# Splitting the second expert's first matrix during the routing, with its lower halves on GpSimd, and putting the last two attention outputs ahead of the transposes

## The chip, the core and the metric

The kernel runs on one core of a Trainium2 chip. Its engines work side by side: TensorE (PE, with its weight loads as PEld), VectorE (DVE), ScalarE (ACT), GpSimd (POOL) and SyncE (SP, which only issues transfers here). The metric is device time in microseconds (us), the median of several runs. Lower is better.

## The reference

```python
# attention: B, H, S, D = 4, 8, 768, 48
cur = einsum('bhd,bhe->bhde', u * kt, vt)
y[:, :, t] = einsum('bhd,bhde->bhe', rt, state + cur)
state = w * state + einsum('bhd,bhe->bhde', kt, vt)
# mixture of experts: 3072 tokens of 384 values, 8 experts, 384 tokens each
logits = x @ w_gate
...   # greedy: largest logit first, each token once, each expert at most 384 tokens
out[mask] = relu(x[mask] @ w1[e]) @ w2[e]
# dense part, on every token
h = maximum(maximum(x @ v1, x @ v2), x @ v3)
out = h @ w_out
```

The outputs of the attention are the rows x. Which expert gets a row depends on the logits of all 3072 rows, so no expert can start before the attention and the routing are over.

## The kernel before, in words

**Attention (`Attention.run`).** 24 steps, one for each block of 128 positions of one batch. A step `i` works on several blocks at once: it loads block i+4 (SP), lets GpSimd scale three operands of the blocks ahead (`decayed` L129, `natural` L184, `bonus` L192 and L193), transposes keys (`turn`, L213), makes the score matrix of block i+1 (`scores`: PE writes pA at L227, DVE masks it into am at L230), takes block i-1 through PE transposes into xt (`cross`: PE L302, ACT L304 and L305), issues four matmuls on ones that nobody reads (`keep`, L237), makes the output of block i (`rows`: PE writes pY at L248, DVE adds two halves into x at L263), adds the logits of block i-2 (`gate`, L313) and updates the state (`state`, L281 and L285, not in the last four steps). pA and pY have two buffers each per pair of tiles, pX has one. After the loop come `cross(23)`, `gate(22)`, `gate(23)` and the copy of all logits into raw (ACT, L359).

**Side work (`Feed`).** The weights are split into an upper and a lower f16 half. The work for this is a list of small pieces with a cost each, and four slots of every step take pieces as fast as the list is due (`due` spreads the summed cost over the steps). One matrix of an expert (`weight`) gives four pieces that sum squares (`look`, ACT L623), three that turn the maximum into a scale, and seven (first matrix) that split: piece n lets ACT write the upper half of part n (`upper`, L690) and DVE the lower half of part n-1 (`lower`, L694, one scalar_tensor_tensor: raw * s - upper, on 128x512). The list of the attention ends with the first matrix of expert 1, `X.weight(1, 0)`, so its six lower halves come last. The raw weights lie in four staging buffers; a load into one waits until its last reader is done.

**Routing (`Routing`).** Three rounds and `settle`, one chain of small DVE, PE and ACT instructions on a table of 128x192 logits, at whose end stand the ids (L1347), by which POOL gathers the rows (L876). At the end of a round `aside` takes pieces from the second list (`Experts.plan`): two, two and none, all `look` pieces of the second matrix of expert 1. In `settle` POOL multiplies into col (L1328) and makes five of the 24 row matrices (L1339).

**Experts (`Experts.run`).** For each expert four products on PE (L919, L1014), with the remaining side work in slots `side`. Each takes from a budget `feed.spare`, from which every piece that runs takes its cost (`Feed.run`); `flush` runs everything that must be done by then. Before the third product of expert 0 the last dense matrix, V[2] (`double(2)`), must be split: ACT L788, DVE L791.

Of the kernel before, what the change touches and what calls it, by code (L numbers as in the profile page):

```python
# [12 lines left out]
OP = mybir.AluOpType  # L13
# [7 lines left out]
NT = B * NC  # L21
# [16 lines left out]
KEEP = 4  # L38
# [6 lines left out]
class Attention:  # L45
# [270 lines left out]
    def run(self, feed):  # L316
        nc = self.nc
        self.load(3)
        feed.ahead(2)
        for i in range(2):  # L320
            self.turn(i)
        self.scores(0)
        self.extra(0)
        for i in range(NT):
            if i == 2:
                self.routing.prepare()

            def side(j):
                if i:
                    feed.spare = 0.0  # L330
                    feed.take(9, min(0.9, feed.due((4 * (i - 1) + j) / (4 * (NT - 4)))), j)

            self.load(i + 4)
            self.across(i + 3)
            self.store(i - 1)
            self.decayed(i + 2)
            self.natural(i + 3)
            self.bonus(i + 2)
            side(1)
            self.turn(i + 2)  # L340
            self.fade(i - 1)
            side(2)
            self.scores(i + 1)
            self.extra(i + 1)
            side(3)
            self.cross(i - 1)
            self.keep(KEEP)
            self.rows(i)
            self.gate(i - 2)
            side(4)  # L350
            self.state(i)
        while feed.left(9):
            feed.run()
        self.store(NT - 1)
        self.cross(NT - 1)
        self.gate(NT - 2)
        self.gate(NT - 1)
        K = self.K
        nc.scalar.activation(K.raw, self.lg, AF.Copy, scale=-1.0)  # L359
# [232 lines left out]
class Experts:  # L592
# [53 lines left out]
    def mark(self, st):  # L646
        st["sent"] = self.feed.now

    def weight(self, e, which, routed=False):

        nc = self.nc
        st = {"sent": 0.0}
        if which == 0:
            src, kb, n, store = self.w1d, self.KD, F, self.W1
            blocks = [self.block(src, e * DM * F + j * 512, [[F, 128], [128 * F, kb], [1, 512]], False)
                      for j in range(2)]
        else:
            src, kb, n, store = self.w2d, self.KF, DM, self.W2
            blocks = [self.block(src, e * DM * F + j * 4 * 128 * DM, [[DM, 128], [128 * DM, 4], [1, DM]], False)
                      for j in range(2)]  # L660

        def look(j):
            def go():
                if j == 0:
                    st["peaks"] = self.wp.tile([128, 4], F32, name=f"wpeak{which}")
                self.square(blocks[j // 2].get()[:, j % 2 * 768:j % 2 * 768 + 768], st["peaks"][:, j:j + 1])
                if j == 3 and not (self.early or routed):
                    self.mark(st)
            return go

        def column(out):
            nc.vector.tensor_reduce(out, st["peaks"], AX.X, OP.max)

        def powers(top):
            yield from self.sc.powering(top, 3, True, st)
            st["w"] = self.wpool[e % 2].tile([128, 2, kb, n], F16, name=f"w{which}", bufs=1)
            store[e] = (st["w"], st["f"])

        def part(j, q):
            if which == 0:  # L680
                return blocks[j].get()[:, q * 512:q * 512 + 512], [st["w"][:, t, q, j * 512:j * 512 + 512] for t in range(2)]
            k = 4 * j + 2 * q
            return blocks[j].get()[:, q * 768:q * 768 + 768], [
                st["w"][:, t, k:k + 2].rearrange("p k n -> p (k n)") for t in range(2)]

        parts = [(j, q) for j in range(2) for q in range(3 - which)]

        def upper(n):
            raw, (hi, _) = part(*parts[n])
            nc.scalar.activation(hi, raw, AF.Copy, scale=st["s"])  # L690

        def lower(n):
            raw, (hi, lo) = part(*parts[n])
            nc.vector.scalar_tensor_tensor(lo, raw, st["s"], hi, op0=OP.mult, op1=OP.subtract)  # L694

        def split(n):
            def go():
                if n < len(parts):
                    upper(n)
                if n:  # L700
                    lower(n - 1)
            return go

        def uses(n):
            return [blocks[parts[i][0]] for i in (n - 1, n) if 0 <= i < len(parts)]

        looks = [(look(j), False, [blocks[j // 2]], 0.9) for j in range(4)]
        if routed:
            self.later = lambda: self.across(column, powers)
        return (looks + ([] if routed else self.scaled(st, column, powers, blocks))  # L710
                + [(split(n), st if n == 0 and not self.early else False, uses(n), 0.6 + 0.3 * which)
                   for n in range(len(parts) + 1)])

    def double(self, i):

# [129 lines left out]
    def plan(self, late):  # L845

        feed = self.feed = Feed(12)
        self.early = False
        parts = [(0.2, self.weight(1, 1, True), None)] + [(1, self.double(i), 0) for i in late]
        parts[-1] = (1, parts[-1][1] + [(self.common, False, [], 1.5)], None)  # L850
        parts.append((1.5, self.double(3), 0))
        for e in range(2, E):
            parts += [(e, self.weight(e, 0), 7), (e + 0.3, self.weight(e, 1), 6)]
        feed.chain(parts)
        feed.close()
        feed.fill()

    def open(self, ctx):
# [259 lines left out]
class Routing:  # L1118
# [88 lines left out]
    def round(self, src, T, n=0):  # L1207

        nc, psum, RW, J, nl = self.nc, self.psum, self.RW, self.J, self.nl
# [38 lines left out]
        for n0, n1, a, c in ((0, V, -1.0, float(N - CAP)), (V, 2 * T, -2.0, float(2 * (N - CAP) - (J * W - 1)))):  # L1248
            nc.vector.tensor_scalar(goal[:RW, n0:n1], po[:RW, 32:33].to_broadcast([RW, n1 - n0]), a, c, op0=OP.mult,
                                    op1=OP.add)  # L1250
        junk = [self.small(f"junk{s}", [128, T + 2, J * W], BF16) for s in range(2)]
        rank = self.small("rank", [128, 2 * T])
        for a in range(2 * T):
            s, t = divmod(a, T)
# [3 lines left out]
            else:  # L1258
# [7 lines left out]
                                       op1=OP.is_equal, accum_out=pick[:RW, 1:2])  # L1266
# [7 lines left out]
                                       op1=OP.mult)  # L1274
        nc.tensor.matmul(pt[:, :E], pick[:RW, 0:1].to_broadcast([RW, 128]), self.same[:RW, :E], start=False, stop=True)
        self.idle(1 if src is self.K.raw else 3)
        self.aside((2, 2, 0)[n])
        pen = self.small("pen", [128, NT, E])
        nc.vector.tensor_tensor(pen, src, pt[:, None, :E].to_broadcast([128, NT, E]), OP.is_gt)
        nc.vector.scalar_tensor_tensor(nl, pen, BIG, src, op0=OP.mult, op1=OP.add)  # L1280
# [161 lines left out]
@with_exitstack  # L1442
def body(ctx, tc, r, rt, k, v, w, u, wg, w1, w2, v1, v2, v3, wo, out, dbg=None):
    nc = tc.nc
    ctx.enter_context(tc.manual_schedule())
    K = Consts(ctx, tc)
    dram = ctx.enter_context(tc.tile_pool(name="dram", bufs=1, space=DRAM))
    x_dram = dram.tile([N, DM], F32, name="x_rows")
    X = Experts(ctx, tc, K, w1, w2, (v1, v2, v3), wo, x_dram, out)
    routing = Routing(ctx, tc, K)  # L1450
    feed = Feed()
    for which in range(2):
        feed.add(0, X.weight(0, which))
    for i in EARLY:
        feed.add(0, X.double(i))
    feed.add(0, X.weight(1, 0))
    feed.close()
    with ExitStack() as actx:
        A = Attention(actx, tc, K, r, rt, k, v, w, u, wg, x_dram,
                      lambda: X.wp.tile([128, 1536], F32, name="stage", bufs=Feed.SLOTS), routing)  # L1460
        X.sc.psum = lambda: A.psum.tile([128, 3, C], F32, name="pX").rearrange("p j n -> p (j n)")
        A.run(feed)
    X.tokens(ctx)
    X.plan([i for i in range(3) if i not in EARLY])
    with ExitStack() as rctx:
        routing.run(rctx, X.inputs(), X.aside, X.sc, lambda: X.gather(0))
    X.open(ctx)
    X.run()
# [44 lines left out]
```

## Time and profile before

| | us |
|---|---|
| median of 3 runs | 688.36 |
| lowest, highest | 687.89, 694.27 |
| the profiled execution, its own time | 689.38 |
| its span, first to last instruction | 687.7 |
| PE busy | 646.8 (94%) |
| DVE busy | 398.8 (58%) |
| ACT busy | 352.2 (51%) |
| POOL busy | 243.6 (35%) |

The profiled execution takes 1.02 us more than the median; 1.68 us of its time lie outside the span. The attention reaches from 0 to about 161 us, the routing to 192 us (ids), the experts start their matmuls at about 197 us. Shares of busy time over the whole span mix these stages; the stages are to be read one by one.

### The profile page before, as it was taken

What the parts mean: (1) busy time and instruction counts of PE and PEld (TensorE: products, weight loads), DVE (VectorE), ACT (ScalarE), POOL (GpSimd) and SP (SyncE); (2) the same over time, 40 slices, a digit from 0 to 9 for tenths busy, and PEclk for the clock granted to TensorE, in tenths of its full rate; (3) what the DMA queues carried; (4) which work ended last, traced back from release to release, by engine and by line L of the source; (5) the groups of instructions that cost most, each with busy time, mean ns of one, the idle gap of its engine ahead of it and who ended that gap; (6) DMA issues with size and microseconds to landing.
All of it is one profiled execution on the core that took longest, in us unless ns stands there. A gap on an engine that the chain in (4) does not pass through costs nothing.

```text
span 687.7 us, 14407 instructions
## 1 busy us (share of the span) xinstructions
PE 646.8 (94%) x5670; PEld 430.1 (63%) x5670; DVE 398.8 (58%) x1048; ACT 352.2 (51%) x785; POOL 243.6 (35%) x270
## 2 busy tenths in 40 slices
PE   7899999997679998899999999999999999999996
PEld 5688787886466564456666656666665666666663
DVE  7787997785745757566366365544636544451321
ACT  3676566643444556466655655546454635442321
POOL 6899999970170003221022123102302111210222
PEclk9999999997569999999999999999999999999999
DMA  7986866615044309026237123412412210000100
GB/s 216 291 261 207 289 211 194 214 49 207 2 135 108 130 5 202 24 63 163 85 83 159 47 69 92 128 47 81 116 46 85 78 47 12 24 0 1 35 2 35
DMA packets 54764, 72.99 MB, mean 106 GB/s; under 512 B 21408, under 2 KB 42016, under 8 KB 54688
## 3 DMA queue, kind: packets, MB, share of 16 engines
q1 hardware_dynamic: 51616, 62.55, 30.6%
q0 software_dynamic: 3072, 9.44, 4.8%
q8 instruction: 46, 0.75, 0.5%
q14 instruction: 30, 0.25, 0.1%
HBM read 58.41 MB, written 9.44 MB: 99 GB/s over the span
## 4 chain that ended last, share of the span: by engine, by line
PE 54%; issue 8%; DVE 4%; ACT 3%; POOL 1%; POOLq 0%; DVEq 0%; ACTq 0%
PE pg L919 25%; PE ps L919 21%; PE px L1014 8%; ACT junk L623 1%; DVE top L996 1%; POOL gt L1001 1%; DVE x2s L977 1%; ACT w L690 1%; ACT gt L1000 0%; DVE ht L949 0%; DVE wo L791 0%; POOL out_dram L1019 0%; DVE gt L763 0%; DVE sc L430 0%; DVE da L747 0%
## 5 line engine op out<-in xcount | busy, mean ns | idle before, releaser
L919 PE MATMUL pg<-x2s,v 128*128 128x384 f16 x1296 | 217.5, 326 | 3.7 <-ACT top L994 3.1
L919 PEld LDWEIGHTS <-v 128*128 128x128 f16 x1296 | 126.8, 98 | 88.3 <-issue 4.8
L1001 POOL TENSOR_TENSOR gt<-top,gt 128x384 f16<-128x384 f32 x48 | 45.2, 941 | 343.5 <-ACT gt L1000 295.4
L919 PEld LDWEIGHTS <-w 128*128 128x128 f16 x1242 | 117.1, 99 | 72.2 <-issue 0.8
L694 DVE SCALAR_TENSOR_TENSOR w<-stage,sc,w 128x512 f16<-128x512 f32 (+1 forms) x80 | 72.7, 934 | 52.1 <-ACT w L690 52.1
L996 DVE SCALAR_TENSOR_TENSOR top<-pg,sc,top 128x384 f32<-128x384 f32 x96 | 59.0, 615 | 73.7 <-PE pg L919 63.6
L919 PE MATMUL ps<-ht,w 128*128 128x384 f16 x576 | 95.1, 326 | 0.1
L919 PE MATMUL ps<-xt,w 128*128 128x384 f16 (+1 forms) x540 | 88.6, 317 | 0.2 <-ACT xt L910 0.2
L1000 ACT ACTIVATE gt<-top 128x384 f16<-128x384 f32 x48 | 25.1, 522 | 111.5 <-DVE top L996 111.5
L1014 PE MATMUL px<-wo,gt 128*128 128x384 f16 x432 | 74.1, 331 | 4.5 <-ACT wo L788 1.6
L690 ACT ACTIVATE w<-stage,sc 128x512 f16<-128x512 f32 (+1 forms) x80 | 61.5, 798 | 6.1 <-DVE sc L468 6.1
L1014 PEld LDWEIGHTS <-gt 128*128 128x128 f16 x432 | 42.4, 99 | 35.1 <-issue 5.4
L623 ACT ACTIVATE junk<-stage 128x768 bf16<-128x768 f32 x64 | 53.6, 838 | 4.2 <-DMA stage<-in_moe_w_dram 3.3
L949 DVE SCALAR_TENSOR_TENSOR ht<-ps,ht 128x384 f16<-128x384 f32 x56 | 31.0, 555 | 32.3 <-ACT ht L948 32.3
L1019 POOL DMA_INDIRECT out_dram<-o,ids x24 | 23.9, 995 | 43.3 <-ACT o L1017 43.3
L994 ACT ACTIVATE top<-pg,sc 128x384 f32<-128x384 f32 x48 | 27.7, 577 | 19.0 <-PE pg L919 18.5
L960 ACT ACTIVATE x<-ps 128x384 f32<-128x384 f32 x24 | 11.8, 491 | 48.8 <-PE ps L919 48.8
L230 DVE TENSOR_TENSOR am<-pA,mask 128x512 f32<-128x512 f32 x48 | 30.7, 680 | 8.9 <-PE pA L227 8.9
L948 ACT ACTIVATE ht<-ps 128x384 f16<-128x384 f32 x56 | 26.8, 482 | 14.9 <-PE ps L919 14.4
L129 POOL TENSOR_TENSOR rt<-rt,tr 128x512 f32<-128x512 f32 x22 | 32.8, 1490 | 0.6 <-DMA rt<-in_rt_dram 0.6
L227 PE MATMUL pA<-rt,kt 64*128 64x128 f32 x384 | 31.9, 304 | 0.6 <-POOL rk L193 0.2
L1017 ACT ACTIVATE o<-px,sc 128x384 f32<-128x384 f32 x24 | 13.9, 580 | 36.1 <-PE px L1014 29.8
(235 smaller groups left out, 871.8 us busy)
## 6 DMA issues: line engine op xcount, KB each, us to landing
stage<-in_moe_w_dram SPq DMA_DIRECT2D x41, 768.0 KB, 5.2
kn<-in_k_dram SPq DMA_DIRECT2D x24, 192.0 KB, 5.2
rn<-in_r_dram SPq DMA_DIRECT2D x24, 192.0 KB, 5.4
v<-in_v_dram SPq DMA_DIRECT2D x24, 192.0 KB, 3.7
rt<-in_rt_dram SPq DMA_DIRECT2D x48, 96.0 KB, 3.6
x_rows<-x SPq DMA_DIRECT2D x24, 192.0 KB, 3.0
stage<-in_moe_w_out_dram SPq DMA_DIRECT2D x3, 768.0 KB, 6.0
xg<-x_rows,ids POOLq DMA_INDIRECT x24, 4.7
```

The source lines that it names most:

```text
L129: (engine or self.nc.gpsimd).tensor_mul(self.RT[i], self.RT[i], self.tr)
L227: nc.tensor.matmul(pa[s][:, j, :], kt[FULL[s], j * C:(j + 1) * C], rt[FULL[s], j * C:(j + 1) * C], start=True, stop=True, skip_group_check ...
L230: nc.vector.tensor_mul(am[:, s], pa[s], self.mask[:, None, :].to_broadcast([128, NP, C]))
L623: self.nc.scalar.activation(self.K.junk, x, AF.Square, accum_out=total)
L690: nc.scalar.activation(hi, raw, AF.Copy, scale=st["s"])
L694: nc.vector.scalar_tensor_tensor(lo, raw, st["s"], hi, op0=OP.mult, op1=OP.subtract)
L919: nc.tensor.matmul(p[:, rows], w[:, wi, k, cols], x[:, xi, k, rows], start=k == 0 and wi + xi == 0, stop=k == kb - 1 and xi == 1, skip_gro ...
L949: nc.vector.scalar_tensor_tensor(h[:, 1, f], p, 0.0, h[:, 0, f], op0=OP.max, op1=OP.subtract)
L994: nc.scalar.activation(t, p, AF.Copy, scale=self.ratio[i])
L996: nc.vector.scalar_tensor_tensor(t, p, self.ratio[i], top, op0=OP.mult, op1=OP.max)
L1001: nc.gpsimd.tensor_sub(gt[:, 1, g], top, gt[:, 0, g])
L1014: nc.tensor.matmul(p, gt[:, gi, g, a * 128:(a + 1) * 128], self.WO[:, wi, g, :], start=g == 0 and gi + wi == 0, stop=g == self.KG - 1 and ...
```

## The change

The pieces that split the first matrix of expert 1 leave the attention's list. `weight(1, 0, left=True)` keeps its looks and its scale there and puts the seven split pieces aside in `held`; `plan` inserts them into the second list behind its four looks, and gives the two staging buffers that hold this matrix to the second list. The rounds take 3, 4 and 4 pieces, so that the four looks and all seven split pieces run in the routing. The lower halves no longer are one DVE instruction each but two on GpSimd: a tensor_scalar that multiplies the raw weights in place, and a tensor_sub. In the attention's last two steps `rows(i)` stands before `cross(i-1)`, and `keep` is left out.

```diff
@@ Attention.run
-            self.cross(i - 1)
-            self.keep(KEEP)
-            self.rows(i)
+            if i < NT - 2:
+                self.cross(i - 1)
+                self.keep(KEEP)
+                self.rows(i)
+            else:
+                self.rows(i)
+                self.cross(i - 1)
             self.gate(i - 2)
@@ Experts.weight
-            nc.vector.scalar_tensor_tensor(lo, raw, st["s"], hi, op0=OP.mult, op1=OP.subtract)
+            if left:
+                nc.gpsimd.tensor_scalar(raw, raw, st["s"], None, op0=OP.mult)
+                nc.gpsimd.tensor_sub(lo, raw, hi)
+            else:
+                nc.vector.scalar_tensor_tensor(lo, raw, st["s"], hi, op0=OP.mult, op1=OP.subtract)
...
+        if left:
+            self.held, splits = (blocks, splits), []
+        return looks + ([] if routed else self.scaled(st, column, powers, blocks)) + splits
@@ Experts.plan
         feed.chain(parts)
+        blocks, splits = self.held
+        feed.plan[4:4] = [(0.1,) + x for x in splits]
+        for b in blocks:
+            b.first = None
         feed.close()
+        feed.blocks = blocks + [b for b in feed.blocks if b not in blocks]
+        feed.loaded = len(blocks)
         feed.fill()
@@ Routing.round
-        self.aside((2, 2, 0)[n])
+        self.aside((3, 4, 4)[n])
@@ body
-    feed.add(0, X.weight(1, 0))
+    feed.add(0, X.weight(1, 0, left=True))
```

DVE, the end of the attention, before (am: masked scores, bon: sums of the bonus, x: the output of a block, w: a half of the split matrix):

```order
L263 TENSOR_TENSOR x<-pY,bv 128x4x48 x2
L694 SCALAR_TENSOR_TENSOR w_2511<-stage,sc_2504,w_2511 128x512 x3
L230 TENSOR_TENSOR am<-pA,mask 128x512 x2
L201 TENSOR_REDUCE bon<-rk 128x8
L694 SCALAR_TENSOR_TENSOR w_2511<-stage,sc_2504,w_2511 128x512
L263 TENSOR_TENSOR x<-pY,bv 128x4x48 x2
L694 SCALAR_TENSOR_TENSOR w_2511<-stage,sc_2504,w_2511 128x512 x2
L230 TENSOR_TENSOR am<-pA,mask 128x512 x2
L201 TENSOR_REDUCE bon<-rk 128x8
L263 TENSOR_TENSOR x<-pY,bv 128x4x48 x4
```

and the same place of the change:

```order
L263 TENSOR_TENSOR x<-pY,bv 128x4x48 x2
L411 TENSOR_REDUCE sc_2566<-pX 1x1
L458 TENSOR_SCALAR sc_2581<-pX 128x1
L465 TENSOR_SCALAR sc_2585<-sc_2581 128x1
L467 TENSOR_SCALAR sc_2585<-sc_2585 128x1
L472 TENSOR_SCALAR sc_2583<-sc_2585 128x1
L472 TENSOR_SCALAR sc_2584<-sc_2585 128x1
L230 TENSOR_TENSOR am<-pA,mask 128x512 x2
L201 TENSOR_REDUCE bon<-rk 128x8
L263 TENSOR_TENSOR x<-pY,bv 128x4x48 x2
L230 TENSOR_TENSOR am<-pA,mask 128x512 x2
L201 TENSOR_REDUCE bon<-rk 128x8
```

The six lower halves between the last masks and outputs are gone; the seven small instructions that make the scale stand one step later than before.

PE, the last step of the attention and what follows it, before (pX<-identf,x: cross; lg<-onesf: keep, whose last pair is shown; pY: rows; lg<-wg: gate):

```order
L302 MATMUL pX<-identf,x 128x128 x3
...
L237 LDWEIGHTS onesf
L237 MATMUL lg<-onesf 128x256
L248 MATMUL pY<-S_119,rt_109 64x64 x16
L248 MATMUL pY<-v_123,am 64x64 x16
L313 MATMUL lg<-wg,xt 128x8 x3
L302 MATMUL pX<-identf,x 128x128 x3
L313 MATMUL lg<-wg,xt 128x8 x6
```

and of the change:

```order
L248 MATMUL pY<-S_119,rt_109 64x64 x16
L248 MATMUL pY<-v_123,am 64x64 x16
L302 MATMUL pX<-identf,x 128x128 x3
L313 MATMUL lg<-wg,xt 128x8 x3
L302 MATMUL pX<-identf,x 128x128 x3
L313 MATMUL lg<-wg,xt 128x8 x6
```

`rows(23)` now stands ahead of `cross(22)`, and the four keep matmuls are gone; step 22 changed in the same way.

POOL between the attention and `settle`, in the change (stage: the raw weights, w: the lower half; col: `settle`). Before, col followed bv directly:

```order
L203 TENSOR_TENSOR bv<-v_123,bon 128x384
L699 TENSOR_SCALAR stage<-stage,sc_2583 128x512
L700 TENSOR_TENSOR w_2590<-stage,w_2590 128x512
L699 TENSOR_SCALAR stage<-stage,sc_2583 128x512
L700 TENSOR_TENSOR w_2590<-stage,w_2590 128x512
...
L1344 TENSOR_TENSOR col<-col,tokf 128x6x24
L1355 TENSOR_SCALAR row<-i_150,bf,tokf 128x128 x5
```

Six such pairs stand there. On ACT the six upper halves (three at the end of the second round, three at the end of the third) and the looks, three and one instead of two and two, are all that the routing gains; on SP one load into a staging buffer fewer stands before the flag of the routing.

## Rows read from the trace of the kernel before

**Rows 1.** Windows by stage: bounds, length, engines' busy us (count), clock, DMA.

```profile
140.00:161.00 21.00, 19.94 (x377) 17.34 (x376) 14.49 (x29) 10.41 (x27) 11.78 (x11) 1.00 0.13 41
161.00:192.00 31.00, 19.85 (x107) 15.21 (x108) 21.81 (x120) 12.93 (x48) 4.57 (x6) 0.55 0.27 103
```

**Rows 2.** Timeline of PE, end of the attention: start, us, instruction, idle before.

```profile
145.07 1.16 PE L227 MATMUL pA<-rt,kt 64*128 64x128 f32 x16
...
148.78 0.84 PE L313 MATMUL lg<-wg,xt 128*128 128x8 f32 x6
149.84 1.55 PE L227 MATMUL pA<-rt,kt 64*128 64x128 f32 x16 [0.22 <-POOL rk L193]
151.97 0.52 PE L302 MATMUL pX<-identf,x 128*128 128x128 f32 x3 [0.59 <-DVE x L263]
152.33 0.60 PE L237 MATMUL lg<-onesf 128*128 128x256 bf16 x4
...
156.41 0.69 PE L248 MATMUL pY<-S,rt 64*64 64x64 f32 x32
...
159.05 0.52 PE L302 MATMUL pX<-identf,x 128*128 128x128 f32 x3
```

**Rows 3.** Timeline of DVE, same stretch.

```profile
144.52 4.46 DVE L694 SCALAR_TENSOR_TENSOR w<-stage,sc,w 128x512 f16<-128x512 f32 x3
148.90 1.27 DVE L230 TENSOR_TENSOR am<-pA,mask 128x512 f32<-128x512 f32 x2
...
151.22 0.61 DVE L263 TENSOR_TENSOR x<-pY,bv 128x192 f32<-128x192 f32 x2
151.75 1.44 DVE L694 SCALAR_TENSOR_TENSOR w<-stage,sc,w 128x512 f16<-128x512 f32 x2
```

**Rows 4.** Timeline of POOL, the same instruction without and beside L694 on DVE.

```profile
140.27 1.27 POOL L129 TENSOR_TENSOR rt<-rt,tr 128x512 f32<-128x512 f32 x1
...
145.29 1.72 POOL L129 TENSOR_TENSOR rt<-rt,tr 128x512 f32<-128x512 f32 x1
```

**Rows 5.** Timeline of DVE, early in the attention.

```profile
27.43 0.96 DVE L1190 TENSOR_SCALAR gone<-same 128x8 f32<-128x8 f32 x1
```

**Rows 6.** Timeline of POOL at that time.

```profile
27.25 1.12 POOL L192 TENSOR_TENSOR rk<-rn,kn 128x384 f32<-128x384 f32 x1
```

**Rows 7.** Groups of POOL's instructions: busy us, mean ns of one, idle before.

```profile
L1001 POOL TENSOR_TENSOR gt<-top,gt 128x384 f16<-128x384 f32 x48 | 45.2, 941 | 343.5 <-ACT gt L1000 295.4 <-issue 48.1
...
L1339 POOL TENSOR_SCALAR row<-i,bf,tokf 128x128 f16<-128x128 f16 x5 | 4.1, 836 | 0.0
...
L76 POOL MEMSET rt<- 128x512 f32 x3 | 1.5, 526 | 0.0
```

**Rows 8.** Timeline of DVE in the routing, end of round 2 to `settle`.

```profile
174.84 0.36 DVE L1280 SCALAR_TENSOR_TENSOR nl<-pen,nl 128x192 f32<-128x192 f32 x1
...
175.62 0.36 DVE L1218 TENSOR_TENSOR no<-nl,best 128x192 bf16<-128x192 f32 x1
...
180.00 0.16 DVE L1271 SCALAR_TENSOR_TENSOR val<-hit,top 96x8 f32<-96x8 f32 x1
...
180.21 0.22 DVE L1273 SCALAR_TENSOR_TENSOR pick<-pick,least 96x1 f32<-96x1 f32 x1
...
183.82 0.27 DVE L1301 TENSOR_SCALAR ahead<-later,heldc 96x200 f16<-96x200 f16 x1
```

**Rows 9.** Timeline of ACT: in round 2; before the third product of expert 0.

```profile
172.56 0.83 ACT L623 ACTIVATE junk<-stage 128x768 bf16<-128x768 f32 x1
...
244.99 2.58 ACT L788 ACTIVATE v<-wo,sc 128x768 f16<-128x768 f32 x3
...
248.80 0.20 ACT L961 ACTIVATION_READ_ACCUMULATOR junk<-ps 128x1 f32 x1
```

**Rows 10.** Timeline of POOL in `settle`.

```profile
187.05 0.44 POOL L1328 TENSOR_TENSOR col<-col,tokf 128x144 f16<-128x144 f16 x1 [31.29 <-ACT gap L1335]
```

**Rows 11.** Timeline of PE, third product of expert 0.

```profile
247.84 13.33 PE L919 MATMUL pg<-x2s,v 128*128 128x384 f16 x81
```

More of the change, by code (lines that the diff above doesn't have):

```diff
@@ L647, in mark, with weight @@
         st["sent"] = self.feed.now
-    def weight(self, e, which, routed=False):
+    def weight(self, e, which, routed=False, left=False):
         nc = self.nc
@@ L709, in weight @@
             self.later = lambda: self.across(column, powers)
-        return (looks + ([] if routed else self.scaled(st, column, powers, blocks))
-                + [(split(n), st if n == 0 and not self.early else False, uses(n), 0.6 + 0.3 * which)
-                   for n in range(len(parts) + 1)])
+        splits = [(split(n), st if n == 0 and not self.early else False, uses(n), 0.6 + 0.3 * which)
+                  for n in range(len(parts) + 1)]
+        if left:
+            self.held, splits = (blocks, splits), []
+        return looks + ([] if routed else self.scaled(st, column, powers, blocks)) + splits
     def double(self, i):
```

## Prediction

> **What bounds the kernel now.** I read the windows by stage first, then the timelines of PE, DVE, ACT and POOL over the end of the attention and over the routing, then the groups of POOL's instructions, because only GpSimd gets a new kind of work. From about 197 us on the experts' matmuls set the pace (PE is busy for 94% of the span). The change acts mainly on the two stages before that. At the end of the attention PE is busy for 19.94 of 21 us and POOL for 11.78. In the routing PE is busy for 19.85 of 31, at a granted clock of 0.55, nearly its 1.2 GHz level, and DVE for 21.81 [rows 1]: a chain of small instructions, each waiting for the one before, with DVE its main carrier. POOL has 4.57 us of work there, none before col at 187.05, where its row shows 31.29 us of idle time [rows 10]. So the routing has a free engine, but no free time on its chain: whatever delays a DVE instruction of the chain delays the ids and all behind them.
>
> **The attention's end.** Six lower halves lie on DVE between 144.52 and about 153.2 us, three of them in 4.46 us and the last two in 1.44 [rows 3]. The first three push the masking for step 22 to 148.90 [rows 3]. For this PE's score matmuls at 149.84 take 1.55 us instead of 1.16, and the next transposes wait for x and start at 151.97 [rows 2]. Without the six, scores(23) may start when gate(19) is through, 148.78 + 0.84 = 149.62, and end at about 150.75: the tail starts 1.2 us earlier than at 151.97. In each of the last two steps keep falls away, which holds PE from 152.33 to 152.86, 0.53 us up to the next matmuls by the spacing of its rows (0.60 long with overlap [rows 2]); two of them give 1.1. With rows ahead of cross, rows(23) no longer waits for the copies of cross(22); that is about one set of transposes, 0.5 us [rows 2], and the set then costs up to 0.2 between rows(23) and cross(23). So rows(23) starts near 153.5 instead of 156.41, and cross(23) near 156.3 instead of 159.05 [rows 2]: **-2.7 us**. The bounds: -1.1 if only keep goes, -3.5 if the stalls of the middle shrink too. The same other side work is done by x(20) in both orders, only spread a little thinner, so I put the middle at nothing, with 2 us either way as its bounds. The seven small instructions of the scale come one step later, a step that has no state to make; what they cost there (about 0.4 us of PE) they no longer cost in the step before. The granted clock is 1.00 in this stretch [rows 1], and PE stays as busy there without keep's idle work, so I charge nothing for that.
>
> **POOL's new work.** It starts when the second round's pieces run. Before, the looks began at 172.56 on ACT and took 0.83 each [rows 9]; now one look and three upper halves stand there, and the first upper half is done at about 174.2. ACT has its next turn on the chain later than it needs for the rest, so its additions cost nothing; if they did, each is below 0.8 us. Per lower half POOL gets a subtraction on 128x512 and a multiplication in place on 128x512. The subtraction lies between 0.94 for 384 columns [rows 7] and 1.27 for a two-input f32 instruction of 512 [rows 4]: I take 1.2. No row shows the multiplication. From below: a memset of the same size, which reads nothing, 0.53 [rows 7]. From above: the one tensor_scalar of POOL, 0.84 for 128 columns with two operations [rows 7], which by columns would be 3.3. It has one input where the 1.27 has two and the memset none, so I take the middle of these two, 0.9. Six pairs make 12.6 us.
>
> The Trainium skill (GPSIMD Engine Reference, Performance versus the Vector engine) gives 769 ns for 512 elements in its best loop; by it, as an estimate, the pairs would make 11.8 us and the sum below would be about 0.3 us smaller.
>
> From 174.2 that ends near 187 to 189, with the wait for ACT's fourth upper half in the third round. col, at 187.05 before, moves by what follows here, to about 191.7, so POOL is not late for it at 0.9.
>
> **What POOL's work does to DVE.** This is the term that turns the sign. At 27.43 DVE took 0.96 us for eight columns; POOL's multiplication on 384 columns ran from 27.25 to 28.37, and DVE's ended with it [rows 5, 6]. Three lower halves beside POOL took 4.46 us, 1.49 each; the last two, mostly clear of it, 1.44 together [rows 3]; POOL's own 1.27 became 1.72 [rows 4]. So a DVE instruction with two inputs in SBUF, or one of the fast copies and tensor_scalars, waits until the POOL instruction under way is over, and then slips in before POOL's next one; the two additions into x, with one input in PSUM, kept their 0.61 in the same stretch [rows 3], and I count such instructions as free. On the chain of the routing, from 174.8 on, nine DVE instructions are of this sort: nl and no, then spread, hit, val and pick, again nl and on, and ahead (five of them in [rows 8]). Each lasts 0.16 to 0.36 us alone [rows 8], so its own length matters little: it pays the rest of a POOL instruction of 0.9 or 1.2 us. I walked both queues forward in turn, POOL's next instruction starting when DVE's is done: nl 0.3, no 0.6, spread 0.75, hit 0 (POOL then waits for ACT), val 0.9, pick 1.1 (directly behind val, it meets a whole subtraction), nl 0.35, on 0.4, ahead 0.3. That is **+4.7 us**. By the same walk a multiplication of 0.53 makes 3.8, one of 1.27 about 6, one of 3.3 about 17.
>
> **Behind the routing.** The budget of the side slots is lowered by each piece that runs, so the seven moved pieces (0.6 each, 4.2 in all) leave it deeper in debt, and V[2] is split later: its three upper halves no longer stand on ACT at 244.99 ahead of the last copy of the second product, but behind it, from about 249.0 [rows 9]. They take 2.58 us, to 251.6, and DVE's third lower half ends near 252.6. PE starts the third product at 247.84 and makes nine matmuls in 13.33/9 = 1.48 [rows 11], so it reaches V[2] at 250.8 and lacks it for about 1 us: **+1.0**, between 0 (if the pieces come as before) and 1.8 (if PE waits for the last half at once). The loads of the second list come later too, but V[2]'s second block is needed only some 10 us after its buffer is free, and no gather is behind it on SP; nothing, or below 1 us if it meets the gather.
>
> **Sum.** -2.7 + 4.7 + 1.0 = +3.0 us. The profiled execution took 689.38, so 692.4 against it; the median of the runs is 1.02 lower, 688.36, and gives **691.4 us**.
>
> **Rivals.** *DVE does not wait*: POOL's new instructions read through what DVE leaves free, or fall in the gaps in which the chain is on PE. For it: three of the nine cost me 0.3 or less, and PE is busy for 19.85 of the 31 us [rows 1], while DVE waits. Against it: an instruction of eight columns that took 0.96 us [rows 5, 6]. Then -2.7 + 0 + 1.0 = -1.7, 686.7 us. *The multiplication is dear*: POOL's only tensor_scalar needs 0.84 for 128 columns [rows 7]. If its time goes by columns, each wait can last 3.3 us, the six pairs 27 us, and col waits for POOL as well as DVE. It decides from about 2 us for one. Then -2.7 + 17 + 1.0 = +15, 703.7 us: clearly slower. For it: same engine, same operation. Against it: two operations there, one here. The Trainium skill (GPSIMD Engine Reference, Engine selection) has elementwise work with two inputs on GpSimd about twice as slow as on VectorE, and with one input roughly at line rate; by that this rival would fall away, but no row here shows one input. *The attention's end does not move*: what held PE was POOL (its row at 149.84 names rk, 0.22 us [rows 2]) and not DVE. Then keep alone gives -1.1, and -1.1 + 4.7 + 1.0 = +4.6, 693.0 us; the wait at 151.97, put down to x on DVE [rows 2], speaks against it.
>
> **Numbers.** Chances: my forecast 0.55 (its own range 689 to 695: the walk between 3.8 and 6, the attention between -3.5 and -1.7, V[2] between 0 and 1.8), no waits on DVE 0.2, dear multiplication 0.13, the end not moved 0.07, something else 0.05. The range 685.5 to 696.5 takes in the forecast, the first and the third rival, and leaves out most of the second and the rest. A change below about 1%, 6.9 us, cannot be told from none by a measurement of this kernel: faster would be below 681.5, which no case gives and only a much better middle of the attention would, 0.03; slower is above 695.2, the dear multiplication and the edge of the forecast, 0.16; the same 0.81.
>
> **What would show it.** In the changed profile: cross(23) at 156 to 157 and the copy to raw some 2 us after it; POOL's tensor_scalar near 0.9 and its tensor_sub near 1.2; val and pick lasting 0.5 us and more where they last 0.16 and 0.22 now [rows 8]; a routing, from raw to ids, longer by 4 to 6 us than the 31 of before [rows 1]; a gap on PE of about 1 us before V[2]. I am wrong if val and pick keep their length while POOL is busy, or if one POOL instruction exceeds 2 us.

## The result and the profile after

The changed kernel takes 693.52 us (median of 6 runs, 691.36 to 696.82) against 689.55 of the kernel before beside it (6 runs): a ratio of 1.0059, 95% interval 1.0036 to 1.0082. It is 4.0 us slower; 691.4 was predicted, with 685.5 to 696.5 as the range. The profiled execution of the change took 691.36, the quickest of its six, so the profiled pair differs by only 2.0 us.

Each stage of the profiled pair, from the PE, ACT and DVE rows that bound it (cross(20), the fourth set of transposes from the attention's end, began at 146.16 before):

| stage | before | after | difference | predicted |
|---|---|---|---|---|
| start to cross(20) | 146.16 | 143.40 | -2.76 | 0, bounds 2 either way |
| cross(20) to raw | 14.87 | 12.06 | -2.81 | -2.7 |
| raw to ids | 30.99 | 35.29 | +4.30 | +4.7 |
| ids to the experts' first matmul | 5.36 | 5.27 | -0.09 | 0 |
| from there to the third product of expert 0 | 50.46 | 48.99 | -1.47 | 0 |
| third product of expert 0 | 31.17 | 34.30 | +3.13 | +1.0 |
| fourth product of expert 0 | 12.05 | 13.75 | +1.70 | 0 |

From there to the end the distance stays 2.0 us. The routing runs from the copy to raw (ACT) to the ids (DVE); its last matmuls wait for col, which DVE begins and POOL multiplies. These rows of before (POOL's is in [rows 10]):

```profile
161.03 0.33 ACT L359 ACTIVATE raw<-lg 128x192 f32<-128x192 f32 x1 [0.42 <-PE lg L313]
...
185.99 0.76 DVE L1325 TENSOR_TENSOR col<-af,i 128x576 f16<-128x576 f16 x1
...
192.02 0.18 DVE L1347 TENSOR_SCALAR ids<-pn 128x24 int32<-128x24 f32 x1 [2.23 <-PE pn L1346]
```

The windows by stage, after, with the columns of [rows 1]: the attention's end, the routing from raw to ids, and the first 10 us of the experts' matmuls:

```profile
140.00:161.00 21.00, 18.88 (x326) 16.51 (x322) 11.10 (x44) 7.28 (x27) 8.88 (x10) 0.92 0.34 115
155.46:190.75 35.29, 20.42 (x107) 15.73 (x108) 24.59 (x121) 16.58 (x54) 20.91 (x18) 0.53 0.25 89
196.02:206.02 10.00, 9.38 (x148) 8.88 (x149) 8.60 (x13) 7.97 (x13) 7.38 (x6) 1.00 0.62 201
```

From raw to ids POOL went from 4.57 to 20.91 us and DVE from 21.81 to 24.59. Of DVE's 2.78 more, 2.16 are the 13 row matrices that it makes in `settle` (5.29 us instead of 3.13), beside POOL's last pairs; they ended before POOL's five, which come last. PE at the attention's end, after (answers to [rows 2]; start, us, instruction):

```profile
143.40 0.55 PE L302 MATMUL pX<-identf,x 128*128 128x128 f32 x3
...
146.78 1.16 PE L227 MATMUL pA<-rt,kt 64*128 64x128 f32 x16
147.87 0.69 PE L248 MATMUL pY<-S,rt 64*64 64x64 f32 x32
...
149.58 0.55 PE L302 MATMUL pX<-identf,x 128*128 128x128 f32 x3
...
153.46 0.55 PE L302 MATMUL pX<-identf,x 128*128 128x128 f32 x3
```

The score matmuls take 1.16 us again, where 1.55 and a wait for x stood before, and no row of this stretch has an idle time. POOL in the routing, after (answers to [rows 10]): the first, second and third pair, the sixth, and col.

```profile
168.93 1.57 POOL L699 TENSOR_SCALAR stage<-stage,sc 128x512 f32<-128x512 f32 x1 [18.30 <-ACT w L694]
170.59 1.15 POOL L700 TENSOR_TENSOR w<-stage,w 128x512 f16<-128x512 f32 x1
171.72 1.56 POOL L699 TENSOR_SCALAR stage<-stage,sc 128x512 f32<-128x512 f32 x1
173.36 1.15 POOL L700 TENSOR_TENSOR w<-stage,w 128x512 f16<-128x512 f32 x1
174.49 1.56 POOL L699 TENSOR_SCALAR stage<-stage,sc 128x512 f32<-128x512 f32 x1
...
184.83 1.15 POOL L700 TENSOR_TENSOR w<-stage,w 128x512 f16<-128x512 f32 x1
185.94 0.43 POOL L1344 TENSOR_TENSOR col<-col,tokf 128x144 f16<-128x144 f16 x1
```

The six pairs run from 168.93 to 185.98 without a gap, and col follows with no idle time in its row: 30.48 us after raw, 26.02 before. DVE at that time, after (answers to [rows 8]):

```profile
171.94 0.57 DVE L1248 TENSOR_TENSOR spread<-top,mine 96x96 f32<-96x96 f32 x1
...
174.86 0.34 DVE L1281 SCALAR_TENSOR_TENSOR hit<-rank,goal 96x8 f32<-96x8 f32 x1
...
175.24 0.16 DVE L1287 SCALAR_TENSOR_TENSOR val<-hit,top 96x8 f32<-96x8 f32 x1
...
175.44 0.22 DVE L1289 SCALAR_TENSOR_TENSOR pick<-pick,least 96x1 f32<-96x1 f32 x1
...
181.36 0.76 DVE L1341 TENSOR_TENSOR col<-af,i 128x576 f16<-128x576 f16 x1
```

val and pick keep 0.16 and 0.22, though POOL is busy; spread and hit, and bi in `settle`, pay 0.32, 0.18 and 0.14, in all 0.64. DVE's own part of col comes 25.90 us after raw, 24.96 before: DVE is 0.94 late, POOL 4.46. PE, after: what the chain then waits for, and the experts.

```profile
186.43 0.18 PE L1362 MATMUL pn<-col,row 128*128 128x24 f16 x1 [2.33 <-POOL col L1344]
...
248.69 0.68 PE L935 MATMUL pg<-x2s,v 128*128 128x384 f16 x3 [0.27 <-ACT v L798]
249.96 0.82 PE L935 MATMUL pg<-x2s,v 128*128 128x384 f16 x4 [0.59 <-DVE v L801]
...
279.31 0.32 PE L1030 MATMUL px<-wo,gt 128*128 128x384 f16 x1 [2.34 <-ACT wo L798]
...
283.78 9.44 PE L1030 MATMUL px<-wo,gt 128*128 128x384 f16 x47 [1.34 <-DVE wo L801]
```

V[2] is late by 0.27 + 0.59 us, and so is W_out behind it: 2.34, where the same row had 1.60 before, and 1.34 where it had 0.61. The last of these waits as it was before, and the windows of the fourth product, before in the first line and after in the second (columns as in [rows 1]):

```profile
284.40 6.82 PE L1014 MATMUL px<-wo,gt 128*128 128x384 f16 x41 [0.61 <-DVE wo L791]
```

```profile
279.01:291.06 12.05, 10.71 (x54) 5.77 (x54) 7.40 (x25) 3.79 (x6) 3.10 (x6) 0.86 0.08 29
279.31:293.06 13.75, 11.68 (x55) 6.07 (x55) 7.41 (x25) 3.79 (x6) 3.09 (x6) 0.75 0.07 26
```

In the third product the granted clock is 1.00 before and after, and of its +3.13, 2.38 are idle time of PE (6.42 us instead of 4.04). The fourth is different: its last wait ends 4.47 us after its start (5.39 before) with six matmuls more to do, and at the spacing of before (41 in 6.66 us) the 47 would end at 12.1 us, an estimate, as long as before. The +1.70 goes with the granted clock, 0.75 instead of 0.86. On ACT, after (answers to [rows 9]):

```profile
246.06 2.58 ACT L798 ACTIVATE v<-wo,sc 128x768 f16<-128x768 f32 x3
...
278.32 1.76 ACT L798 ACTIVATE wo<-gt,sc 128x768 f16<-128x768 f32 x2 [1.69 <-DVE sc L472]
281.80 0.92 ACT L798 ACTIVATE wo<-gt,sc 128x768 f16<-128x768 f32 x1
```

The upper halves of V[2] begin 1.05 us after the third product, 2.85 ahead of it before; the third upper half of W_out stands apart from the first two and later, where all three stood together.

### The profile page after: what moved, and what is told of

The parts are those of the page before. It is cut to its first block, busy times and chain, and to the rows that moved or that the text cites. A ratio compares the mean times of both kernels' runs of the same rounds, so it can differ in the third digit from the quotient of the medians.

```text
span 689.6 us, 14396 instructions
## 1 busy us (share of the span) xinstructions
PE 642.5 (93%) x5662; PEld 425.7 (62%) x5662; DVE 395.8 (57%) x1042; ACT 352.6 (51%) x785; POOL 257.6 (37%) x282
## 4 chain that ended last, share of the span: by engine, by line
PE 56%; issue 8%; DVE 3%; ACT 3%; POOL 1%; POOLq 0%; DVEq 0%; ACTq 0%
PE pg L935 26%; PE ps L935 22%; PE px L1030 8%; DVE top L1012 1%; POOL gt L1017 1%; ACT junk L627 1%; ACT w L694 1%; ACT gt L1016 0%; DVE v L801 0%; DVE da L764 0%; POOL out_dram L1035 0%; DVE gt L773 0%; DVE x2s L993 0%; DVE sc L434 0%; ACT x2s L992 0%
## 5 line engine op out<-in xcount | busy, mean ns | idle before, releaser
L702 DVE SCALAR_TENSOR_TENSOR w<-stage,sc,w 128x512 f16<-128x512 f32 (+1 forms) x74 | 66.2, 920 | 53.6 <-ACT w L694 53.6
L694 ACT ACTIVATE w<-stage,sc 128x512 f16<-128x512 f32 (+1 forms) x80 | 61.5, 799 | 9.5 <-DVE sc L472 9.5
L215 ACT ACTIVATE kt<-pT 128x512 f32<-128x512 f32 x24 | 14.3, 596 | 38.3 <-PE pT L213 38.2
L129 POOL TENSOR_TENSOR rt<-rt,tr 128x512 f32<-128x512 f32 x22 | 31.0, 1411 | 0.0
```

Source lines behind the costliest of these rows:

```text
L129: (engine or self.nc.gpsimd).tensor_mul(self.RT[i], self.RT[i], self.tr)
```

## The experiments

| run | median us (runs) | before beside it | ratio, 95% interval |
|---|---|---|---|
| the change | 693.52 (6) | 689.55 | 1.0059, 1.0036 to 1.0082 |
| 1 order alone | 689.60 (12) | 689.82 | 0.9998, 0.9982 to 1.0013 |
| 2 move alone | 696.31 (6) | 689.82 | 1.0107, 1.0080 to 1.0135 |
| 3 budget given back | 690.22 (11) | 689.82 | 0.9995, 0.9983 to 1.0007 |
| 4 lower halves on DVE | 693.95 (5) | 689.82 | 1.0059, 1.0040 to 1.0078 |
| 5 one round earlier | 690.30 (11) | 690.87 | 1.0000, 0.9983 to 1.0016 |
| 6, 7, 8 | 693.59, 689.93, 693.00 (1 each) | 690.87 | |
| 9 behind the routing | 686.85 (12) | 689.17 | 0.9962, 0.9943 to 0.9982 |
| 10 the same, with keep | 685.94 (12) | 689.82 | 0.9960, 0.9939 to 0.9981 |

**1. The order of the last two steps alone.** The kernel before, with this hunk and nothing else:

```diff
-            self.cross(i - 1)
-            self.keep(KEEP)
-            self.rows(i)
+            if i < NT - 2:
+                self.cross(i - 1)
+                self.keep(KEEP)
+                self.rows(i)
+            else:
+                self.rows(i)
+                self.cross(i - 1)
```

> The kernel before with one part of the change alone: in the attention's last two steps rows goes ahead of cross and keep is left out; the split of expert 1 stays in the attention and on VectorE. In the profiled change the copy to raw came 5.57 us earlier, 2.8 of it before cross(20) and 2.8 after. If the order of the last two steps makes the second half and the thinner side work the first: raw 1 to 3 us earlier than the kernel before, total about 687.5 (-1.1 for keep to -2.8), routing and experts as before. Rival, the six lower halves on VectorE are what holds the tail and the order is worth little: raw less than 0.8 us earlier, total as before.

raw came 1.94 us earlier, which by itself is the first theory's number; but 1.20 of it lie ahead of cross(20), where the profiles spread by more than that. cross(20) to raw took 14.13 us (14.87 before): -0.74. raw to ids took 31.58, +0.59, all of it ahead of the first hit, and the total stayed, as the rival has it. The order is worth little while the lower halves lie on VectorE.

**2. The move alone.** The change, with that hunk undone:

```diff
-            if i < NT - 2:
...
-            else:
-                self.rows(i)
-                self.cross(i - 1)
```

> The change without its part on the attention's last two steps: cross, keep and rows stand as before, the split of expert 1 is in the routing with its lower halves on GpSimd. If the move costs what the pair of profiles says (routing +4.3, experts +3.3, against -2.8 from the middle of the attention and -1 at its tail): total 3.5 to 5 us above the kernel before, about 693 to 694.5. Rival, the tail's gain came from the missing lower halves and not from the order: total as the change, +2.

The total was 7.4 us above before by its ratio, more than either theory gave. cross(20) to raw 13.55 (-1.32), raw to ids 35.31, third and fourth product 34.28 and 15.06. So the tail's -2.81 needs both parts: -0.74 and -1.32 make only -2.06. And the third and fourth product lose 6.1 us here, 4.83 in the change; the granted clock over the fourth is 0.66 here.

**3. The budget given back.** The change, with one line at the start of `Experts.run`:

```diff
+        feed.spare += 4.2
         self.gather(1)
```

> The change with 4.2 added to the side work's budget at the start of the experts, the cost of the seven pieces that were moved into the routing; from the routing on every engine's order is then that of the kernel before. If the experts lose by the debt of this budget (third and fourth product of expert 0 +3.13 and +1.70, the stretch before them -1.47): V[2] is split at the old place, those two products take 31.2 and 12.1 us again, the total is 3.0 to 3.6 us below the change. Rival, they lose by the clock or by contention that the later start brings: the two products stay long and the total stays within 1 us of the change.

The two products took 31.14 and 12.06 us, those of before to 0.03. PE and ACT of this run around the third product:

```profile
248.70 13.33 PE L935 MATMUL pg<-x2s,v 128*128 128x384 f16 x81
...
279.84 0.32 PE L1030 MATMUL px<-wo,gt 128*128 128x384 f16 x1 [1.60 <-ACT wo L798]
```

```profile
245.84 2.58 ACT L798 ACTIVATE v<-wo,sc 128x768 f16<-128x768 f32 x3
```

V[2] stands 2.86 us ahead of its product again, with 13.33 us of matmuls without a gap as in [rows 11]. By the ratios the run is 0.64% (4.4 us, some 1.8 either way, an estimate from the two intervals) quicker than the change: that much the debt cost, and the 3.0 to 3.6 expected lie within it. The third product shows it without spread: 34.27 to 34.30 us in all six profiles with the debt, 31.12 to 31.17 in the six without.

**4. The lower halves on DVE.** The change, with this in `lower`:

```diff
-            if left:
+            if False:
                 nc.gpsimd.tensor_scalar(raw, raw, st["s"], None, op0=OP.mult)
```

> The change with the six lower halves of the routing as one VectorE instruction each, as they were in the attention, and nothing of them on GpSimd. If GpSimd's queue is what makes the ids late (col waits for the last subtraction): col's multiplication follows VectorE's comparison at once, and VectorE's chain pays instead for 6 lower halves of 0.72 and the waits for ACT's upper halves in rounds 2 and 3; raw to ids 33 to 36 us, within 1.5 us of the change either way. If VectorE's instructions were made late by GpSimd's (the reason in the prediction) and these waits cost more than the lower halves themselves: raw to ids 32 us or less, total 3 us or more below the change.

raw to ids took 34.68 us (35.29 in the change), the total that of the change: as a place GpSimd was about as dear as VectorE. DVE's rows are the whole price, 4.15 us of lower halves between the small instructions; DVE's part of col comes 3.67 us later than before:

```profile
170.26 1.42 DVE L702 SCALAR_TENSOR_TENSOR w<-stage,sc,w 128x512 f16<-128x512 f32 x2
...
178.84 2.73 DVE L702 SCALAR_TENSOR_TENSOR w<-stage,sc,w 128x512 f16<-128x512 f32 x4
```

**5. One round earlier.** Run 3, with five splits ahead of the looks:

```diff
-        feed.plan[4:4] = [(0.1,) + x for x in splits]
+        feed.plan[4:4] = [(0.1,) + x for x in splits[5:]]
+        feed.plan[0:0] = [(0.1,) + x for x in splits[:5]]
...
-        self.aside((3, 4, 4)[n])
+        self.aside((5, 4, 2)[n])
```

> The change with the budget given back (the 4.2 of the run before) and the seven split pieces taken one round earlier: five in the first round ahead of the four looks, which all go to the second round, two in the third. GpSimd gets the same six pairs, some 8 us earlier after raw. If GpSimd's queue is late for col: its last subtraction ends at about raw + 23, col's multiplication follows VectorE's comparison at once at about raw + 27, raw to ids is 31.5 to 32.5 instead of 35.3, and the total lies about 3 us below the run with the budget alone, at 687, 2 to 3 us below the kernel before. Rival, VectorE's instructions pay for GpSimd's wherever these stand: the same waits move into the first two rounds, raw to ids stays at 34.5 to 35.5, the total at 690.

The rival won: raw to ids 35.37, the total as run 3. (The third product took 31.12 us as in run 3, the fourth 13.80 at a granted clock of 0.75, so the fourth can lose its time without the debt too.) POOL and then DVE of this run:

```profile
161.34 1.57 POOL L699 TENSOR_SCALAR stage<-stage,sc 128x512 f32<-128x512 f32 x1 [10.88 <-ACT w L694]
163.00 1.15 POOL L700 TENSOR_TENSOR w<-stage,w 128x512 f16<-128x512 f32 x1
...
169.78 1.56 POOL L699 TENSOR_SCALAR stage<-stage,sc 128x512 f32<-128x512 f32 x1
...
185.60 0.43 POOL L1346 TENSOR_TENSOR col<-col,tokf 128x144 f16<-128x144 f16 x1 [4.65 <-DVE col L1343]
```

```profile
161.46 0.57 DVE L1291 SCALAR_TENSOR_TENSOR pick<-pick,least 96x1 f32<-96x1 f32 x1
...
163.10 1.26 DVE L1298 SCALAR_TENSOR_TENSOR nl<-pen,raw 128x192 f32<-128x192 f32 x1
...
169.87 0.62 DVE L1289 SCALAR_TENSOR_TENSOR val<-hit,top 96x8 f32<-96x8 f32 x1
...
184.71 0.76 DVE L1343 TENSOR_TENSOR col<-af,i 128x576 f16<-128x576 f16 x1
```

POOL is no longer late: it waits 4.65 us for DVE. But DVE is: nine instructions (pick, nl, spread, hit, val, nl, spread, pick, nl) last 4.15 us longer in all than alone, and DVE's col comes 29.42 us after raw. Who meets a subtraction lasts until it is over: nl to 164.36, the subtraction to 164.15. Who meets a multiplication is through some 0.7 us after its start: pick at 162.03, 0.69 after 161.34; val at 170.49, 0.71 after 169.78.

**6. Only the subtractions.** The change without one line:

```diff
-                nc.gpsimd.tensor_scalar(raw, raw, st["s"], None, op0=OP.mult)
```

> The change without GpSimd's six multiplications (the lower halves of expert 1's first matrix are then wrong by the scale); the six subtractions stay. If VectorE waits only in the first 0.7 us of a multiplication: spread, hit and bi take 0.25, 0.16 and 0.18 as before, and with 6 x 1.15 us of work GpSimd is in time for col: raw to ids 31 to 31.5. If it waits for the subtractions with their two inputs (the reason in the prediction): some of the nine instructions still take 0.3 us more than before, raw to ids 32 to 33.

33.36 us, a little over the second theory's number. DVE of this run, beside subtractions that reach from 170.94 to 174.55 and from 177.40 to 180.81:

```profile
172.73 0.81 DVE L1233 TENSOR_TENSOR no<-nl,best 128x192 bf16<-128x192 f32 x1
...
177.61 0.99 DVE L1288 SCALAR_TENSOR_TENSOR pick<-pick,least 96x1 f32<-96x1 f32 x1
```

With two nl these pay 1.95 us. The first theory, waits in the multiplications alone, is wrong. This run and the next leave out part of the split and are one execution each, so only their rows count.

**7. Only the multiplications.**

```diff
-                nc.gpsimd.tensor_scalar(raw, raw, st["s"], None, op0=OP.mult)
-                nc.gpsimd.tensor_sub(lo, raw, hi)
+                nc.gpsimd.tensor_scalar(lo, raw, st["s"], None, op0=OP.mult)
```

> The change without GpSimd's six subtractions: the multiplication writes the scaled matrix as f16 where the lower half belongs, so these halves hold something else. If VectorE waits in the first part of a multiplication: instructions that meet a start take 0.3 us more, about 0.5 to 1 us in all; GpSimd's 6 x 1.6 us end before col: raw to ids 31.5 to 32.2. If the multiplication does not hold VectorE up: no longer instruction, raw to ids 31.

It doesn't decide. Writing a place of its own, the multiplication no longer waits for ACT's upper half, and the six ran earlier than meant, three before raw (155.83) and three into the first round. POOL, and DVE in that round:

```profile
150.98 9.27 POOL L699 TENSOR_SCALAR w<-stage,sc 128x512 f16<-128x512 f32 x6
```

```profile
156.58 0.36 DVE L1233 TENSOR_TENSOR no<-raw,best 128x192 bf16<-128x192 f32 x1
...
158.08 0.30 DVE L1247 TENSOR_TENSOR spread<-top,mine 96x144 f32<-96x144 f32 x1
```

no and spread, 0.96 and 0.93 us after the start of a multiplication, took their usual time, and none met a start; raw to ids was 31.50. It shows one thing beside: three such instructions under the attention's last 5 us leave cross(20) to raw at 12.07.

**8. keep put back.** The change, with one line more:

```diff
                 self.rows(i)
                 self.cross(i - 1)
+                self.keep(KEEP)
```

> The change with keep's four matmuls put back into the attention's last two steps, behind cross; rows stays ahead of cross. From the matmuls of cross(20) to raw the change takes 12.06 us, the kernel before 14.87, the order alone 14.13. If keep costs its 0.53 on PE in each step, as the prediction says: 13.1. If PE stands still there anyway and only the order counts: 12.0 to 12.3. The routing as in the change, 35.3.

cross(20) to raw 12.76: keep costs 0.70 for both steps, between the two theories. raw to ids 34.97.

**9. Behind the routing.** Run 3, with lower halves on DVE as in run 4, and the pieces after `settle`:

```diff
-        self.aside((3, 4, 4)[n])
+        self.aside((2, 2, 0)[n])
...
         for _ in other:
             pass
+        self.aside(7)
         self.aside = lambda pieces: None
```

> The change with the seven split pieces taken after settle instead of in the rounds, which take two, two and none again as before; the lower halves are one VectorE instruction each, GpSimd gets none; the budget is given back (4.2); the attention's end is that of the change. In the kernel before ACT has nothing from its last row (about 190) to 198.42 and VectorE nothing from 193.81 to 199.03, while the gather runs: six upper halves (3.9 us) and six lower halves (6 x 0.72 = 4.3 us) fit in there. If the routing's +4.3 is paid only because the pieces stand on or beside its chain: raw to ids 31 to 31.6, ids to the first matmuls of the experts 4.6 to 5.4 as before, the products as in the run with the budget alone, the total 686 to 687, 3 to 4 us below the kernel before. Rival, the split takes a wait elsewhere: VectorE's lower halves run beside GpSimd's gather instructions and make the first transposed tokens late, or V[2]'s raw weights, whose staging buffers come free some 10 to 20 us later, arrive late for their place in the first product: 2 to 4 us more in the experts, the total 689 to 691.

686.85 us, 0.38% below the kernel before (0.18 to 0.57%) and 1% below the change. ACT and DVE of this run, from the ids on:

```profile
188.75 3.78 ACT L694 ACTIVATE w<-stage,sc 128x512 f16<-128x512 f32 x6 [0.68 <-PE pn L1363]
...
197.30 1.09 ACT L926 ACTIVATE xt<-px,sc 128x384 f16<-128x384 f32 x2 [3.63 <-PE px L917]
```

```profile
190.23 0.18 DVE L1364 TENSOR_SCALAR ids<-pn 128x24 int32<-128x24 f32 x1 [2.23 <-PE pn L1363]
...
191.94 4.05 DVE L702 SCALAR_TENSOR_TENSOR w<-stage,sc,w 128x512 f16<-128x512 f32 x6
197.92 1.14 DVE L927 SCALAR_TENSOR_TENSOR xt<-px,sc,xt 128x384 f16<-128x384 f32 x2 [1.92 <-ACT xt L926]
```

All six lie in the time in which both engines wait, from the end of their part of `settle` to the gathered rows: DVE still waits 1.92 us behind them, ACT 3.63. raw to ids 31.54 (the first hit comes 0.56 later than before, the rest is as before), the two products 31.15 and 12.06. Of the rival a little is there: ids to the first matmul took 6.03 us, 5.36 before.

**10. The same, with keep.** Run 9 with the line of run 8 (`+ self.keep(KEEP)`), to see whether keep holds up the clock.

> The run before this with keep's four matmuls back in the attention's last two steps, behind cross. In the profiles so far the tail, cross(20) to raw, takes 12.06 us without keep and 12.76 with it; in the first 6 us after raw the granted clock was 0.70 to 0.76 in three kernels with keep and 0.53 to 0.54 in five of the eight without, and the first hit then came 5.44 to 5.75 us after raw instead of 5.94 to 6.03. If keep holds the clock up over the last steps: clock 0.7 or more in these 6 us, raw to ids 31.0 instead of 31.5, the tail 12.8, and the total the same within 0.5 us. If the clock falls by chance and not by keep: 0.53 and 31.5 again, the total 0.7 us above the run before.

In this execution it doesn't. The window of the first 6 us after raw, in this run, columns as in [rows 1]:

```profile
156.43:162.43 6.00, 3.93 (x17) 3.21 (x17) 4.30 (x25) 2.64 (x12) 0.00 (x0) 0.53 0.64 236
```

The granted clock is 0.53 with keep, 0.54 in run 9; raw to ids 31.56 and 31.54. So keep alone doesn't hold the clock; whether it makes a fall less likely one profile can't tell. When the clock falls after raw varies between the profiles, at a price of up to 0.6 us, and what decides it stays open. Runs 9 and 10 can't be told apart by time.

## Why the prediction was right, and where not

The total lay in the range and the sign of the sum held, but the sum came near in part by luck: the routing's term was met by another mechanism, and a gain ahead of cross(20) that was put at nothing stood against a loss in the experts that was sized too small.

**The attention's end, -2.7: right.** -2.81, and cross(20) to raw took 12.06 or 12.07 us in all seven profiles with this order, without keep and without the lower halves on VectorE there. The split of it was off: keep is worth 0.70 for both steps (run 8), not 1.1; the lower halves, once the order is changed, 14.13 - 12.06 = 2.07, not 1.2; and the parts are worth more together than alone (runs 1, 2). **The middle, 0:** -2.76 in the profiled pair, but ten profiles with the split moved have cross(20) at 143.11 to 146.62, 144.2 on average, and the two with it in place 144.96 and 146.16. Some 1.3 us may be real; the runs don't tell it from their own spread.

**The routing, +4.7: near in size (+4.30), by another way.** Two steps failed, and together they gave the number. The first is the walk: it let nine DVE instructions pay 4.7 us, and in the change three paid 0.64, while val and pick kept their length, which the prediction itself had named as a sign of being wrong. The second is "POOL is not late for it at 0.9". The subtraction was 1.15 to 1.24, as taken (1.2), the multiplication 1.56 to 1.75 instead of 0.9; both ends of the bracket, 0.53 and 3.3, held, the choice between a memset and the two-input row didn't. Six pairs made 17 us, and col, on the same queue, came straight behind them, 4.46 us later than before. By the prediction's own start, 174.2, 17 us end at about 191.2, an estimate, still ahead of its 191.7 for col: POOL was late because the pairs were longer and DVE was not late. The rival with the dear multiplication had this wait, but put its start at about 2 us for one. The Trainium skill (GPSIMD Engine Reference, section Engine selection) has GpSimd's elementwise work with one input roughly at line rate and with two inputs about twice as slow as VectorE's; here the instruction with one input was the longer one, 1.56 against 1.15.

That DVE waits for POOL is true, but not by the walk's rule that it waits until the POOL instruction is over: this held for subtractions, not for multiplications. Run 5, in which POOL isn't late, pays 4.15 on nine DVE instructions. In the change DVE's small ones fell mostly into the later part of multiplications, where they didn't wait, and DVE lost 0.94, of which 0.32 lie in the first round (granted clock over the first 6 us 0.67, 0.74 before). The change with the budget given back, the same instructions in the same order in the routing, had DVE's col 27.99 us after raw instead of 25.90, and POOL's at 30.57 all the same: DVE's loss depends on how the two queues fall, POOL's queue sets the end. In run 4 the same work on VectorE cost 3.7. So in the rounds it cost about 4 us on either engine.

**Behind the routing, +1.0: the term that was mis-sized.** V[2] itself was late by 0.86 us, as worked out. But the debt doesn't end there: what is put off crowds the rest of the third product, and the wait for W_out ahead of the fourth is 0.74 longer, which the prediction didn't follow; with the smaller waits between them the third product takes 3.13 more. The fourth product's +1.70, put at nothing, goes with the granted clock, 0.75 instead of 0.86. Both products took 4.83 us more; run 3 gives back 4.4 by the ratios. Over the fourth the clock was 0.66 to 0.76 in all six profiles with the debt and 0.86 or 1.00 in five of the six without; run 5 had 0.75, so that the debt lowers it is likely and not shown. The -1.47 ahead of them is no gain of the change: the same stretch took 49.93 to 50.61 in five other kernels with this order behind the routing, and the granted clock at its start was higher in the profiled run (1.00 in the first 10 us, 0.80 before). Runs 2 and 6, also at 1.00 there, took 49.93 and 49.96, so some 0.9 us of it stay unexplained.

**The sum, corrected:** -2.8 - 1.3 + 4.3 + 4.4 = +4.6, against 4.0 measured (2.5 to 5.7). **The clock, nothing charged for keep's going:** no run shows a price; keep alone does not hold the clock (run 10). **The rivals:** that the attention's end doesn't move is wrong (12.06 instead of 14.87). That DVE doesn't wait came near in the change, 0.64, but not as a rule: in run 3, the same order, DVE's part of col was 2.09 us later than in the change, and run 5 paid 4.15.

## What to carry to other kernels

Before side work is moved, count three things: the moved work's own queue up to the next instruction of the chain on it, the waits it causes on the neighbour engine, and every budget or counter that its pieces go through, since a debt there delays work hundreds of matmuls later. A stage with idle engines is not a free place if its chain runs through them; the free place was where the chain waits for a transfer, 5 us between the ids and the gathered rows, and there the same six halves, on DVE, cost some 0.7 us. When two parts of a change gain and lose by a few us each, undo them one at a time: here the sum of +4 hid a gain. Run 9 keeps the attention's part and ends 2.6 us below the kernel before.

## What the runs showed of the hardware

- GpSimd, 128x512, in the change: a multiplication by a scalar per partition, f32 in place, 1.56 to 1.75 us; a subtraction of two inputs into f16, 1.15 to 1.24.
- A small DVE instruction with two inputs in SBUF that comes behind the start of GpSimd's subtraction lasts until that is over, at most 0.22 us longer (run 5: 164.36 and 164.15); reductions kept their length beside it (run 6: 0.35 as alone). One that meets the start of a multiplication was through 0.69 to 0.79 us after it; val, 0.75 us after such a start, took its usual 0.16. The reverse is there too: in the change nl, at 177.31, took its usual 0.36, and the multiplication of 177.27 lasted 1.75 instead of 1.56. The Trainium skill (SBUF — State Buffer, section Who interferes with whom) has one of the two engines wait for the whole instruction of the other; the subtraction agrees, the later part of the multiplication does not, as far as GpSimd's spans in the profile can be trusted.
- GpSimd's gather instructions beside DVE's lower halves took 1.19, 1.31 and 1.01 us in run 9, and 1.20, 0.96 and 0.94 in run 5 without them.
